# Reordering the head of an attention-plus-feed-forward kernel: states ahead of masks, outputs in their own banks, first rows by token blocks

## The chip, the cores and the metric

One core of a Trainium2 chip. The metric is device time in microseconds (us); a run gives one time, and its profile gives a span that is some 2 us shorter (205.6 us for a run of 207.38). Each milestone below is read from the trace of one execution.

## The reference

Linear attention with decay over blocks of 64 tokens, whose output goes into a GELU feed-forward layer.

```python
# attention: B=4, H=8, S=768, D=64
for b in range(S // 64):
    intra = (qb @ kb.T * Dmask) @ vb
    inter = (qb * lam_pow) @ kv_state
    out[b] = intra + inter
    kv_state = lam_block * kv_state + (kb * rev_pow).T @ vb
# feed-forward: x (3072 x 512), w_in (512 x 2048), w_out (2048 x 512)
out = gelu_tanh(x @ w_in) @ w_out
```

## The kernel before

The kernel walks through 24 steps, each of 256 tokens of four heads. Two steps (the two halves of the heads) make 256 rows of the feed-forward layer's input. The helpers that matter:

```python
def scores(n):   ...  # TensorE: q.k of step n into the bank pair Sps
def causal(n):   ...  # VectorE: PT = Sps * mask                        (1.22 us)
def products(n, s, banks=None, evacuate=True):
    # TensorE. n: k.v of step n into columns 256.. of two banks OK[0], OK[1]
    #          s: outputs of step s (PT.v, then q.state) into columns 0..255
    ...
def x_out(s, OK): ... # ScalarE: two copies OK[c] -> xT, the feed-forward input
def update(s, c, parts="tu"):
    # "t", VectorE: state t = t_old * lamu + OK[c][:, 256:384]  (two instructions)
    # "u", GpSimd:  u = t with the other head masked out
def cast_win(j, lo, hi, w, cs, on_act): ...  # w_in from fp32 to fp16, VectorE or ScalarE
def fill(n): ...      # TensorE: the next n pieces of feed-forward work
```

A *row* of the feed-forward layer below (rows 0 to 3, rows 4 to 7) is not a token: it is one block of 128 of the 2048 hidden features, computed in one PSUM bank. A *chunk* is 128 of the layer's 512 inputs, and a *token block* is 256 of the 512 rows of `x` that come first. *Cover* is the TensorE work that runs while another engine's copy is under way.

Every engine executes its instructions in the order of the program. A bank that VectorE (a state) and ScalarE (a copy) both read is handed over by semaphores, one reader after the other. The stretch that the change reorders, before:

```python
    update(1, 0)
    idle(3)
    scores(2)
    products(2, None)
    causal(2)
    prep_v(3)
    update(2, 0)
    update(1, 1)
    update(2, 1, "t")
    idle(2)
    stage_t(3)
    OK1 = products(None, 1, evacuate=False)[0]
    OK2 = products(None, 2, evacuate=False)[0]   # new banks
    x_out(2, OK2)
    x_out(1, OK1)
    scores(3)
    banks = products(3, None)
    update(3, 0)
    cast_win(0, 0, 256, 128, c01)                 # rows 0 and 1, VectorE
    cast_win(0, 256, 512, 256, c01, on_act=True)  # rows 2 and 3, ScalarE
    causal(3)
    queue_group(0)
    fill(4)                                       # rows 0-3, chunks 0 and 1
    products(None, 3, banks)
    cast_win(0, 0, 512, 256, c23)
    fill(8)                                       # rows 0-3, chunks 2 and 3, by token block
    # ... rows 4 to 7, 8 to 15, w_out, then steps 4 to 23
```

Later, nine more pieces of fill, then `prep(4)` (VectorE multiplies step 4's query by its decay, ScalarE casts its keys) and `stage_t(4)`, TensorE's transposes of both.

## Time and profile before

| | before |
|---|---|
| time, median of 3 runs (of 4 with the later rounds) | 207.87 us (207.69) |
| all four | 207.36 to 208.07 us |
| TensorE busy | 197.1 of 205.6 us |
| step 2's scores begin | 13.63 us |
| first feed-forward row begins | 18.15 us |
| rows 4 to 7 begin | 22.54 us |
| step 4's transposes begin | 40.67 us |

Read such a kernel by the matmul starts. TensorE is 96% busy, so an edit that removes no matmuls can only close holes between them. The prediction shows where the holes are. The table's last four rows are starts of single TensorE instructions; they are the milestones.

### The profile page before, as it was taken

To read this page: it belongs to the slowest core of one execution; us is meant where nothing else is said; L and a number is where in the kernel's file an instruction comes from. 1 tells how busy PE (TensorE), PEld (TensorE's weight loads), DVE (VectorE), ACT (ScalarE), POOL (GpSimd) and SP (SyncE) were. 2 spreads that over 40 slices of the span, in tenths; PEclk is the share of its full clock that TensorE was granted. 3 is DMA by queue.
4 is the path that set the end of the run, shared out by engine and by line. 5 is a ranking of instruction groups with operands and counts; after the bars stand their busy time and mean duration, and the time that the engine had idled before them with its cause. 6 is when DMAs were issued, how large, how long until landed. Compare 5 with 4: busy or idle time off the path is not lost.

```text
span 205.6 us, 5583 instructions
## 1 busy us (share of the span) xinstructions
PE 197.1 (96%) x2321; PEld 128.0 (62%) x2321; DVE 144.4 (70%) x271; ACT 108.1 (53%) x204; POOL 69.9 (34%) x80
## 2 busy tenths in 40 slices
PE   7988999999999999999999999999999999999990
PEld 2554644456875788644788554788555888446880
DVE  4788627867699998929997639996559474056631
ACT  2355778475882573487541577442676323665110
POOL 5495123646586851326224403404420110000000
PEclk9999999999999999999999999999999999999999
DMA  5999999999999998996549981736320003300033
GB/s 137 298 322 387 387 387 376 277 291 332 333 248 243 294 235 154 202 279 161 141 102 274 230 234 50 190 70 156 103 54 0 3 0 105 104 0 0 3 102 102
DMA packets 64057, 37.85 MB, mean 184 GB/s; under 512 B 17696, under 2 KB 59168, under 8 KB 64032
## 3 DMA queue, kind: packets, MB, share of 16 engines
q1 hardware_dynamic: 63760, 37.24, 66.9%
q8 instruction: 18, 0.29, 0.6%
q10 hardware_dynamic: 272, 0.26, 0.4%
q14 instruction: 7, 0.06, 0.1%
HBM read 27.27 MB, written 6.29 MB: 163 GB/s over the span
## 4 chain that ended last, share of the span: by engine, by line
PE 91%; DVE 2%; DMA 2%; issue 1%; ACT 1%; DVEq 0%
PE Hps L401 35%; PE O2ps L416 10%; PE MB L469 8%; PE MA L469 7%; PE MD L469 7%; PE Sps L271 4%; PE MC L469 4%; PE Hps L514 4%; PE OK L329 3%; PE idle L573 3%; PE OK L320 3%; PE Tps L242 2%; DMA qkT<-qk 2%; PE OK L306 1%; DVE t L366 1%
## 5 line engine op out<-in xcount | busy, mean ns | idle before, releaser
L401 PE MATMUL Hps<-xT,w_in 128*128 128x512 f16 (+1 forms) x416 | 79.1, 346 | 0.0
L405 ACT ACTIVATE gT<-Hps 128x512 f16<-128x512 f32 x88 | 52.3, 597 | 22.6 <-PE Hps L401 21.8
L401 PEld LDWEIGHTS <-w_in 128*128 128x128 f16 x416 | 40.2, 98 | 33.5
L373 POOL TENSOR_TENSOR u<-t,lumask 128x256 f16<-128x256 f32 x40 | 31.4, 791 | 80.9 <-DVE t L366 54.2
L446 DVE TENSOR_TENSOR gs<-gT 128x512 f16<-128x512 f16 (+1 forms) x70 | 36.6, 586 | 10.8 <-ACT gT L405 10.6
L280 DVE TENSOR_TENSOR PT<-Sps,mask 128x1024 f16<-128x1024 f32 x24 | 29.2, 1217 | 17.3 <-PE Sps L271 17.2
L469 PEld LDWEIGHTS <-gs 128*128 128x128 f16 x360 | 34.9, 98 | 4.0
L211 POOL TENSOR_TENSOR v<-v,dv 128x512 f16<-128x512 f32 x24 | 29.2, 1219 | 4.7 <-DMA v<-in_v_dram 4.7
L343 ACT ACTIVATE xT<-OK 128x256 f16<-128x256 f32 x48 | 18.2, 453 | 20.0 <-PE OK L329 16.5
L416 PE MATMUL O2ps<-w_out,gT 128*128 128x512 f16 x96 | 21.9, 379 | 0.0
L476 ACT ACTIVATE m<-MB 128x512 f32<-128x512 f32 x9 | 5.4, 597 | 28.1 <-PE MB L469 28.1
L226 ACT ACTIVATE qk<-k 128x512 f16<-128x512 f32 x24 | 15.0, 624 | 8.8 <-DMA k<-in_k_dram 8.8
L221 DVE TENSOR_TENSOR qk<-q,dq 128x512 f16<-128x512 f32 x23 | 19.2, 834 | 0.0
L469 PE MATMUL MA<-w_sum,gT 128*128 128x256 f16 x144 | 17.5, 273 | 0.1
L469 PE MATMUL MD<-w_sum,gs 128*128 128x256 f16 x136 | 17.5, 273 | 0.0
L469 PE MATMUL MB<-w_out,gs 128*128 128x256 f16 x144 | 17.2, 273 | 0.0
L366 DVE SCALAR_TENSOR_TENSOR t<-t,lamu,OK 128x64 f32<-128x64 f32 x64 | 14.5, 273 | 2.1 <-PE OK L306 0.9
L480 DVE TENSOR_TENSOR o<-MA,m 128x512 f32<-128x512 f32 x9 | 6.2, 688 | 13.9 <-ACT m L476 13.9
L469 PEld LDWEIGHTS <-gT 128*128 128x128 f16 x144 | 14.0, 98 | 2.8 <-ACT gT L405 0.3
L416 PEld LDWEIGHTS <-gT 128*128 128x128 f16 x96 | 9.2, 98 | 9.9
L271 PEld LDWEIGHTS <-qkT 64*64 64x64 f16 x384 | 6.1, 106 | 8.3 <-issue 4.2
L123 DVE TENSOR_TENSOR w_sum<-wo,wo 128x1024 f16<-128x1024 f32 x6 | 7.9, 1362 | 4.2 <-DMA wo<-in_moe_w_out_dram 4.2
(55 smaller groups left out, 169.2 us busy)
## 6 DMA issues: line engine op xcount, KB each, us to landing
q<-in_q_dram SPq DMA_DIRECT2D x24, 256.0 KB, 4.5
k<-in_k_dram SPq DMA_DIRECT2D x24, 256.0 KB, 5.0
v<-in_v_dram SPq DMA_DIRECT2D x24, 256.0 KB, 4.9
out_dram<-o SPq DMA_DIRECT2D x22, 256.0 KB, 3.4
wo<-in_moe_w_out_dram SPq DMA_DIRECT2D x4, 1024.0 KB, 9.2
wi<-in_moe_w_in_dram SPq DMA_DIRECT2D x4, 512.0 KB, 8.0
wi<-in_moe_w_in_dram SPq DMA_DIRECT2D x2, 1024.0 KB, 12.5
out_dram<-o SPq DMA_DIRECT2D x2, 128.0 KB, 2.2
```

What stands on the lines that cost most here:

```text
L211: pin(nc.gpsimd.tensor_tensor(wide(tv[:]), ld32[s][2][:], decay(dv, s), ALU.mult))
L221: pin(q_eng.tensor_tensor(wide(tq), q32[:], decay(dq, s), ALU.mult))
L226: pin(nc.scalar.activation(out=wide(tk), in_=k32[:], func=AF.Copy))
L280: pin(nc.vector.tensor_tensor(t[:].rearrange("p a b c d -> p (a b) (c d)"), Ss.pop(n)[:].rearrange("p a b c d -> p (a b) (c d)"), mask[:]. ...
L343: pin(nc.scalar.activation(out=dst[:, :, c * P : (c + 1) * P].rearrange("p hp (t j) -> p hp j t", j=2), in_=OK[c][:, 0:256].rearrange("p ( ...
L366: pin(nc.vector.scalar_tensor_tensor(t[:, hp, :], state[half][:, hp, :], lamu[:, 2 * half + hp : 2 * half + hp + 1], K[:, hp, :], ALU.mult ...
L373: pin(nc.gpsimd.tensor_tensor(u[:], state[half][:].unsqueeze(2).to_broadcast([P, 2, 2, D]), lumask[:, 2 * half : 2 * half + 2, :].unsqueez ...
L401: pin(nc.tensor.matmul(by_block(Hps[:, i, :]), w_in16[:, c, f * P : (f + 1) * P], x(c), start=(c == 0), stop=(c == NC - 1)))
L405: pin(nc.scalar.activation(out=dst, in_=Hps[:], func=AF.Gelu_apprx_tanh))
L416: pin(nc.tensor.matmul(O2[tau][0][:], gT[:, f % HF, f // HF, tau * P : (tau + 1) * P], w_out16[:, f, :], start=(n == 0), stop=(n == NF - 1)))
L446: pin(nc.vector.tensor_tensor(gsum[m][:, i, :], block(T0, F0, i), block(T1, F1, i), op))
L469: pin(nc.tensor.matmul(dst, lhsT, rhs, start=(i == 0), stop=(i == HF - 1), skip_group_check=True))
```

## The change

The intent: free VectorE, which carries the chain of waits twice in this stretch. Step 1's second state and step 2's first state go ahead of step 2's mask; step 2's outputs go into the banks that already hold its k.v; the first four feed-forward rows are cut by token block, so that each block can start when its inputs are there; the first weight casts go ahead of step 3's first state (they were ahead of its mask already). Step 3's outputs move behind four of the matmuls on chunks 2 and 3, so that four matmuls instead of eight are left to cover their copies. One later cast goes to ScalarE, and half of step 3's transposes and the second copy of its outputs go to VectorE.

```diff
-        if s == 2:                                   # evacuation of the transposes
+        if s in (2, 3):                              # half on ScalarE, half on VectorE
 ...
-    def x_out(s, OK):
+    def x_out(s, OK, second=None):                   # second copy on another engine
 ...
-            for fs, stages in ((range(4), (((0, 1), both, False), ((2, 3), b0, False),
-                                           ((2, 3), b1, True))),
+            for fs, stages in ((range(4), (((0, 1), b0, False), ((0, 1), b1, False),
+                                           ((2, 3), b0, False), ((2, 3), b1, True))),
 ...
     update(1, 0)
+    update(1, 1, "t")
     idle(3)
     scores(2)
-    products(2, None)
+    banks = products(2, None)
+    update(2, 0)
     causal(2)
     prep_v(3)
-    update(2, 0)
-    update(1, 1)
-    update(2, 1, "t")
+    update(1, 1, "u")
     idle(2)
     stage_t(3)
-    OK1 = products(None, 1, evacuate=False)[0]
-    OK2 = products(None, 2, evacuate=False)[0]
-    x_out(2, OK2)
-    x_out(1, OK1)
+    products(None, 1)
+    products(None, 2, banks)
+    update(2, 1, "t")
     scores(3)
     banks = products(3, None)
-    update(3, 0)
     c01, c23 = slice(0, 2), slice(2, 4)
     cast_win(0, 0, 256, 128, c01)
     cast_win(0, 256, 512, 256, c01, on_act=True)
+    update(3, 0)
     causal(3)
     queue_group(0)
-    fill(4)
-    products(None, 3, banks)
-    cast_win(0, 0, 512, 256, c23)
     fill(8)
+    cast_win(0, 0, 256, 256, c23, on_act=True)
+    cast_win(0, 256, 512, 256, c23)
+    fill(2)
+    products(None, 3, banks, evacuate=False)
+    x_out(3, banks[0], nc.vector)
+    fill(6)
+    update(3, 1, "t")
     cast_win(1, 0, 512, 256, c01)
-    update(3, 1, "t")
     cast_win(1, 0, 512, 256, c23)
```

More of the change, by code (lines that the diff above doesn't have):

```diff
@@ L244, in stage_t @@
         o = qkp.tile([P, 2, 2, 2, P], FP16, tag="qkT", name=f"qkT_{s}")
-        if s == 2:
+        if s in (2, 3):
             pin(nc.scalar.activation(out=o[:, 0], in_=Tps[:, 0], func=AF.Copy))
             pin(nc.vector.tensor_copy(out=o[:, 1], in_=Tps[:, 1]))
-        elif s in (1, 3, 5, 6):
+        elif s in (1, 5, 6):
             pin(nc.scalar.activation(out=o[:], in_=Tps[:], func=AF.Copy))
@@ L342, in x_out @@
         for c in range(2):
-            pin(nc.scalar.activation(
-                out=dst[:, :, c * P : (c + 1) * P].rearrange("p hp (t j) -> p hp j t", j=2),
-                in_=OK[c][:, 0:256].rearrange("p (hp j t) -> p hp j t", hp=2, j=2),
-                func=AF.Copy))
+            d = dst[:, :, c * P : (c + 1) * P].rearrange("p hp (t j) -> p hp j t", j=2)
+            o = OK[c][:, 0:256].rearrange("p (hp j t) -> p hp j t", hp=2, j=2)
+            if c == 1 and second is not None:
+                pin(second.tensor_copy(out=d, in_=o))
+            else:
+                pin(nc.scalar.activation(out=d, in_=o, func=AF.Copy))
     us = {}
@@ L509, in mm1_part @@
         def mm1_part(f, cs, blocks, last):
-            if cs[0] == 0:
+            opens = f not in first
+            if opens:
                 first[f] = ps_M.tile([P, N], FP32, tag="M", name="Hps")
@@ L515, in mm1_part @@
                                      w_in16[:, c, f * P : (f + 1) * P], x(c)[:, blocks],
-                                     start=(c == 0), stop=last and c == NC - 1,
+                                     start=opens and c == 0, stop=last and c == NC - 1,
                                      skip_group_check=True))
```

## The prediction

> **What bounds the kernel now.** I read the page's busy shares first, then the chain of waits in order of time, then the timeline of the first 25 us engine by engine, then the waits between 12 and 41 us. The page says that TensorE is the kernel:
>
> ```profile
> PE 197.1 (96%) x2321; PEld 128.0 (62%) x2321; DVE 144.4 (70%) x271; ACT 108.1 (53%) x204; POOL 69.9 (34%) x80
> ```
>
> A span of 205.6 less 197.1 leaves 8.5 us in which TensorE is idle. About 1.4 us of it lies before its first instruction and some 5 us after its last matmul, so about 2 us is left, and nearly all of it comes before 19 us. The chain of waits, between 13 and 21 us, shows where (start, length, what):
>
> ```profile
> 13.59 0.04 issue
> 13.63 0.45 PE Sps L271 x16
> ...
> 15.25 0.36 DVE t L366 x2
> 15.61 0.02 issue
> 15.63 0.48 DVE t L366 x2
> 16.11 0.04 issue
> 16.15 0.41 PE OK L320 x15
> ...
> 17.42 0.47 DVE t L366 x2
> 17.89 0.21 DVE w_in L107
> 18.10 0.05 issue
> 18.15 0.60 PE Hps L514 x2
> 18.75 0.04 issue
> 18.79 1.47 PE Hps L514 x6
> ```
>
> The reader is to see that VectorE carries the chain twice: the state of step 1 (`t`, 15.63) holds back step 2's outputs at 16.15, and the state of step 3 (17.42) plus a weight cast hold back the first feed-forward row at 18.15. The TensorE and VectorE timelines give the sizes:
>
> ```profile
> 18.15 2.11 PE L514 MATMUL Hps<-xT,w_in 128*128 128x512 f16 x8 [0.79 <-DVE w_in L107]
> ...
> 17.80 0.93 DVE L107 CAST w_in<-wi 128x256 f16<-128x256 f32 x2
> ...
> 20.86 0.76 ACT L343 ACTIVATE xT<-OK 128x256 f16<-128x256 f32 x2 [2.20 <-PE OK L329]
> ...
> 21.71 0.47 DVE L366 SCALAR_TENSOR_TENSOR t<-t,lamu,OK 128x64 f32<-128x64 f32 x2 [0.51 <-issue]
> ```
>
> From matmul start to matmul start I find four holes after 15 us that a new order could close: 0.19 us at 15.5, 0.32 at 15.8, 0.79 at 17.4 and 0.20 at 18.6, together 1.5 us. After 18.8 us TensorE streams back to back until one hole of 0.2 us at 77 us, which comes from ScalarE's order there. So the change, which lies wholly before 24 us, is worth what it moves the start of that stream, and never more than 1.5 us of 207.9, or 0.7%.
>
> **What the Trainium skill says.** (1) "PSUM — Partial Sum Buffer", section "PSUM bank collisions raise a hardware error", says that any two engines on one bank and quadrant collide, ScalarE reading against VectorE reading included, so that access is guarded by bank. This kernel's build does so, and the trace agrees: the `t` at 21.71 shares its bank with the second `xT` copy of ScalarE, which ends at 21.62, and starts 0.09 us later. (2) "SBUF — State Buffer", section "Who interferes with whom", says that a VectorE cast in a two-port mode and a GpSimd instruction exclude each other. The trace agrees: of the two casts at 17.80 the first took 0.29 us and the second, beside GpSimd's `u` at 17.97, took 0.72. (3) "TensorE: Matmul & The Clock Gate", section "Wait — 56ns, not 53.3ns?", gives N / 2.4 GHz + 2.5 ns between warm matmuls. Here it is 0.216 us at 512 columns and 0.109 at 256, so a row split in two pays some 2 ns for each added matmul.
>
> **The change part by part.** I carried the new instruction order of each engine through with these durations, and 0.05 to 0.09 us for each hand-over, as the trace has them.
>
> State of step 1 ahead of the mask. Its two `t` instructions go to 13.89 (the copy at 13.50 takes 0.28, and its reader follows 0.1 later), and the first state of step 2 to 14.27 to 14.72, since its products end at 14.17. The mask of step 2 then runs 14.64 to 15.86, where it was 14.11 to 15.33. Step 2's outputs now wait for that mask alone, since they go into banks that they already have: 15.92, where they were held to 16.15. That is 0.23 us earlier. Six `t` instructions leave the stretch behind the mask, but half a microsecond of them goes in front of it, so only half of the 0.5 us of holes there is won. The key transposes of step 3 are not in the way: ScalarE's half 15.20 to 15.80, then VectorE's half to 16.24, because they share a bank. Done alone by ScalarE they took to 16.22.
>
> Scores of step 3: 16.59 (was 16.82). Its products end at 17.13 (was 17.36).
>
> ScalarE copies step 1's outputs at 15.78 and 16.10, and step 2's at 16.59 and 16.91, ending at 17.35 (was 18.20). That is 0.85 us won, but off the path. Its weight cast starts at 17.3 instead of 18.01.
>
> VectorE now has the second state of step 2 ahead of the first weight casts. That `t` reads the bank that ScalarE copies until 17.35, so by the bank rule it starts at 17.44 and ends at 17.91. The casts come at 17.83 and 18.04, and now no `u` lies beside them (the next waits for step 3's state), so both should take 0.29. First feed-forward row: 17.83 + 0.29 + 0.05 = 18.17, where it was 18.15. The 0.23 us won is lost here, to a wait that takes the place of the one removed. The second row comes at 18.39, without the 0.20 us hole.
>
> From there: 16 matmuls of 0.109 are 1.75, to 19.92; four more on chunks 2 and 3 make 20.36. ScalarE's cast for those needs the second part of the weights, which landed at 18.61 in the trace; it runs 18.66 to 19.31, in time. Step 3's outputs, 0.58 plus 0.09 for the switch, end at 21.03 (was 20.77). Only four matmuls, 0.44 us, now lie behind them, to 21.47, where eight and 0.87 us did. The second token block needs both copies of step 3's outputs: ScalarE's half 21.12 to 21.58 and VectorE's half 21.24 to 21.64, so it starts at 21.70, a new hole of 0.23 us. Eight matmuls later, at 22.57, rows 4 to 7 begin. Before it was 22.54. VectorE's casts for rows 4 and 5 follow its copy and the last state, and end at 22.52, just in time.
>
> Sum: -0.20 (second row) + 0.02 (first row) + 0.23 (wait for step 3's copies), and the rest in rounding: about 0.0 us. All matmuls are the same work, with 8 more starts of about 2 ns, and 8 more weight loads of 98 ns that lie under matmuls of 109 ns.
>
> **The rivals.** (a) The new order closes the hole: if the second state of step 2 does not wait for ScalarE's copy, the casts start when the weights land (17.26), and the row starts near 17.65; with the late hole smaller too, 0.5 us is won at 22 us. The banks' rule and the 21.71 wait speak against it, and even then the next rival takes part of it back. (b) A fixed arrival caps any gain. The DMA queue is full from 3 us to beyond 45 us, so landings do not move with TensorE:
>
> ```profile
> 38.77 1.50 DVE L221 TENSOR_TENSOR qk<-q,dq 128x512 f16<-128x512 f32 x1
> ...
> 40.46 0.59 PEld L242 LDWEIGHTS <-qk 128*128 128x128 f16 x7
> 40.67 0.50 PE L242 MATMUL Tps<-ident,qk 128*128 128x128 f16 x6
> ```
>
> Step 4's query ends at 40.27 on VectorE, behind sums that started when a weight landed at 32.1, and TensorE takes it at 40.46. An earlier TensorE would wait there: of any gain only 0.15 to 0.3 us can pass. For (a) this makes 207.55 to 207.7. (c) The split rows and the smaller cover behind step 3's outputs cost more than I count, or VectorE's casts for rows 4 to 7 come late (they follow one copy and one state, and the second of them lies beside GpSimd's `u`, where such a cast took 0.84): 0.3 us lost, 208.2. Nothing later gives it back, since TensorE has no later idle time to absorb it.
>
> **Range and chances.** The mean of the three is close to no change: 207.87 + 0.0 by my sum, a little less for (a) under the cap of (b), which I hold likelier than (c) since the last wait is worked out from overlapping copies and may be 0.1 shorter. I take 207.75. The before runs spread over 0.56 us by themselves, which is wider than the effect, so 8 times in 10 it should be within 207.3 to 208.25. A gain of over 2% needs 4.2 us, nearly three times all the holes that the change can reach: 0.01. A loss of over 2% would need a wait of 4 us that nothing shows: 0.01. Within 2%: 0.98.
>
> **What would show it.** In the changed profile: step 2's outputs near 15.9 and scores of step 3 near 16.6; the second state of step 2 just behind the end of ScalarE's fourth copy (about 17.4); the first feed-forward row at 18.1 to 18.2, with both casts at 0.29; a hole of about 0.2 us ahead of the second token block near 21.6; rows 4 to 7 at 22.4 to 22.7; no hole at the transposes of step 4 near 40.5. If the first row starts at 17.7, rival (a) holds and I then expect TensorE to wait for the query at 40.3. If holes appear at 22.6 to 24, rival (c) holds. The prediction is wrong if the time moves by more than 0.6 us either way, which would need a wait outside the first 24 us.

## The result, and the profile after

The changed kernel took 207.74 us (median of 4, 207.47 to 208.02) against 207.69 for the kernel before (median of 4, 207.36 to 208.07). The ratio is 1.0002, with a 95% interval of 0.9977 to 1.0027: the same. Ratios here and below are the mean time of one kernel's fast runs over that of the other's in the same rounds, so they are not quite the ratios of the medians quoted beside them.

The page's busy shares of the changed kernel: TensorE has eight more matmuls (the split rows), VectorE one instruction more (two copies more, one cast less).

```profile
PE 196.8 (96%) x2329; PEld 128.4 (62%) x2329; DVE 144.8 (70%) x272; ACT 108.1 (53%) x204; POOL 70.1 (34%) x80
```

The chain of waits of the changed kernel in the same stretch (start, length, what):

```profile
14.79 1.14 DVE PT L280
15.93 0.04 issue
15.98 0.42 PE OK L320 x16
16.39 0.23 PE OK L329 x2
16.62 0.02 issue
16.65 0.77 ACT xT L348 x2
17.42 0.04 DVEq L368
17.46 0.04 issue
17.50 0.47 DVE t L368 x2
17.97 0.21 DVE w_in L107
18.19 0.05 issue
18.23 2.36 PE Hps L517 x20
20.59 0.35 PE OK L320 x16
20.94 0.34 PE OK L329 x4
21.28 0.02 issue
21.30 0.46 DVE xT L346
21.76 0.05 issue
21.80 2.34 PE Hps L517 x14
```

Where step 2's outputs (15.98) waited for a state before, they now wait for the mask alone, and step 3's scores follow sooner. But the chain no longer goes from TensorE to VectorE. It goes through ScalarE's copies of those outputs (16.65), then a state on VectorE (17.50), then the cast, then the first row (18.23). The VectorE timeline and its waits say the same with the length of the wait:

```profile
17.50 0.47 DVE L368 SCALAR_TENSOR_TENSOR t<-t,lamu,OK 128x64 f32<-128x64 f32 x2 [1.16 <-ACT xT L348]
17.89 0.49 DVE L107 CAST w_in<-wi 128x256 f16<-128x256 f32 x2
```

VectorE is idle for 1.16 us ahead of the state. The state reads columns 256 to 383 of the bank and the copy columns 0 to 255, so what ties them is the bank and not the data. The two casts behind it take 0.49 us together, where one of them took 0.72 alone before, so rows 0 to 3 now run without a hole (20 matmuls in 2.36 us). The second new hole is at the end of the chain: the second token block (21.80) waits for VectorE's copy of step 3's outputs.

The runs differ in when step 2's scores begin, from 13.32 to 14.19 us, although TensorE has the same instructions up to there in every kernel here. So I count the milestones from that start. All numbers in us, from the start times of single TensorE instructions. A hole is the time between two matmul starts above their usual spacing; the brackets of the views count idle time from the modelled end of the matmul before, and so are smaller (0.30 for a hole of 0.46).

| after step 2's scores | before | changed |
|---|---|---|
| step 2's outputs, first | 2.13 (but 15 of 16 wait to 2.51) | 2.25 |
| step 3's scores | 3.19 | 2.93 |
| first feed-forward row | 4.51 | 4.51 |
| step 3's outputs | 6.55 | 6.80 |
| hole ahead of the second token block | none | 0.27 |
| rows 4 to 7 | 8.91 | 8.97 |
| step 4's transposes | 27.04 | 27.10 |
| last matmul | 186.66 | 186.72 |

From step 4's transposes to the last matmul both take 159.62 us. Everything that the change did is over at rows 4 to 7, where it is 0.06 us behind.

### The profile page after: what moved, and what is told of

It reads as the page before. It is cut to its first block, busy times and chain, and to the rows that moved or that the text cites. A ratio compares the mean times of both kernels' runs of the same rounds, so it can differ in the third digit from the quotient of the medians.

```text
span 205.8 us, 5599 instructions
## 1 busy us (share of the span) xinstructions
PE 196.8 (96%) x2329; PEld 128.4 (62%) x2329; DVE 144.8 (70%) x272; ACT 108.1 (53%) x204; POOL 70.1 (34%) x80
## 4 chain that ended last, share of the span: by engine, by line
PE 88%; DMA 3%; SPq 2%; DVE 2%; ACT 2%; issue 1%; DVEq 0%
PE Hps L403 37%; PE O2ps L418 10%; PE MB L471 8%; PE MA L471 7%; PE MD L471 7%; PE MC L471 4%; PE Sps L271 3%; PE Hps L517 3%; PE OK L329 3%; DMA k<-in_k_dram 3%; PE OK L320 3%; SPq L68 2%; PE Tps L242 1%; PE OK L306 1%; ACT xT L348 1%; DVE t L368 1%
```

## The experiments

Theory A: the change wins where it was meant to, and pays it back by two waits, namely the state that waits for ScalarE's copy in the same bank (with the casts queued up behind it), and the thin cover behind step 3's outputs. Theory B: even if these were mended, a later arrival (step 4's query) would cap the gain. Theory C: the first row is bound by something else, such as the landing of the weights. Each run has a profile, and all were correct.

**The state behind the casts.** One line of the changed kernel moved.

```diff
     products(None, 2, banks)
-    update(2, 1, "t")
     scores(3)
     banks = products(3, None)
     cast_win(0, 0, 256, 128, c01)
+    update(2, 1, "t")
```

> The changed kernel with one line moved: the second state of step 2 goes behind the first two weight casts instead of ahead of them. Theory A (that state waits for ScalarE's copy of the same bank and holds the casts back): the first feed-forward row starts when the weights have landed and been cast, 0.5 to 0.6 us earlier after the scores of step 2 (3.9 to 4.0 us instead of 4.51), the hole after step 3's outputs stays at 0.2 to 0.3 us, rows 4 to 7 begin 0.5 to 0.6 us earlier, and the transposes of step 4 pass on 0.4 to 0.5 of that; time 0.3 to 0.5 us below the changed kernel. Theory B (an arrival later on caps every gain): first row earlier as in A, but the transposes of step 4 move by less than 0.2 us and the time stays. Theory C (the casts wait for something else, such as the weights' arrival): the first row does not move by more than 0.1 us.

Measured: 207.17 us (median of 6) against 207.38 before (11 runs); ratio 0.9983, interval 0.9968 to 0.9998. The first row starts at 3.58, rows 4 to 7 at 8.24 (0.73 earlier than in the changed kernel), the last matmul at 186.21 (0.51 earlier, and 0.45 earlier than in the kernel before; the interval of the ratio is 0.04 to 0.66 us). The VectorE timeline of this run:

```profile
17.03 0.71 DVE L107 CAST w_in<-wi 128x256 f16<-128x256 f32 x2 [0.40 <-DMA wi<-in_moe_w_in_dram]
17.80 0.86 DVE L368 SCALAR_TENSOR_TENSOR t<-t,lamu,OK 128x64 f32<-128x64 f32 x4
```

The casts now start as the weights land (17.00). Theory A's first wait is shown: one line in the program's order was worth 0.93 us at the first row, counted from step 2's scores. More than I expected, because scores of step 2 came 0.3 us later in this run than in the changed kernel's while the weights landed 0.2 us earlier; by the clock from the span's start the row came 0.64 us earlier (17.59 against 18.23). C is refuted for the changed kernel. In the six traces in which the state still stands ahead of the casts and the rest of the new head is in place, the first row comes at 4.51 each time, while the weights land anywhere from 16.93 to 17.40; only with the state out of the way can the landing bound the row.

At rows 4 to 7 the gain is 0.73 and not 0.93, because a hole of 0.19 us opens at 18.23, ahead of row 2: ScalarE casts the weights of rows 2 and 3 behind its fourth copy, from 17.55 to 18.17.

```profile
17.55 0.62 ACT L105 ACTIVATE w_in<-wi 128x512 f16<-128x512 f32 x1
```

Theory B, that step 4's transposes move by less than 0.2 us, is wrong: they move by 0.52. A part of it is right: of the 0.73 us at rows 4 to 7, 0.51 arrive. The rest is a wait at step 4's transposes, in the weight-load timeline of this run:

```profile
40.59 0.28 PEld L242 LDWEIGHTS <-qk 128*128 128x128 f16 x5 [0.54 <-DVE qk L221]
```

The query ended on VectorE at 40.53. Between rows 4 to 7 and these transposes lie 18.13 us in the kernel before and in the changed one, and 18.34 here: 0.21 us of TensorE's time was lost. The query's load is not the whole of this cap. It landed at 38.83, and VectorE's multiply of it then took 1.52 us (39.01 to 40.53), beside GpSimd's cast of `w_out` (38.01 to 39.99); the same multiply for step 5 took 0.68. In all 13 traces step 4's takes 1.25 to 1.52. No run here moved that cast, so what this would win is not shown.

**The same, with the transposes asked for later.** First attempt.

```diff
-    fill(9)
+    fill(10)
     prep(4)
     stage_t(4)
     prep(5)
-    fill(2)
+    fill(1)
```

> The run with the state behind the casts, and beside it one more piece of four feed-forward matmuls placed ahead of step 4's transposes instead of behind them, so that TensorE asks for step 4's query 0.86 us later. Theory A without a cap: the same end as the run with the state behind the casts alone, within 0.1 us in the trace. Theory B (the query's arrival on VectorE caps the gain): the last matmul comes 0.1 to 0.4 us earlier than in that run, and there is no wait at the transposes. If the shorter cover behind the transposes (0.86 instead of 1.73 us) is too short, the scores of step 4 wait for the copy of the transposes, up to 0.2 us.

Measured: 208.22 us (median of 6), ratio 1.0029 (1.0013 to 1.0045): a miss. The tenth piece completes an output, and its copy then stands ahead of the cast of step 4's keys in ScalarE's order:

```profile
41.55 0.60 ACT L424 ACTIVATE o<-O2ps 128x512 f32<-128x512 f32 x1 [2.78 <-PE O2ps L418]
...
42.05 1.14 ACT L226 ACTIVATE qk<-k 128x512 f16<-128x512 f32 x2
42.72 0.23 PEld L242 LDWEIGHTS <-qk 128*128 128x128 f16 x4 [1.16 <-ACT qk L226]
```

ScalarE waits for that output, and the keys behind it, so the second half of the transposes comes 1.14 us late. I made the edit blind to what one piece brings along; it is mended below.

**More cover behind step 3's outputs.**

```diff
     fill(8)
     cast_win(0, 0, 256, 256, c23, on_act=True)
     cast_win(0, 256, 512, 256, c23)
-    fill(2)
     products(None, 3, banks, evacuate=False)
     x_out(3, banks[0], nc.vector)
-    fill(6)
+    fill(8)
```

> The changed kernel with step 3's outputs placed four matmuls earlier, so that eight matmuls instead of four lie between them and the second token block. Theory A: the hole of 0.27 us behind step 3's outputs shrinks to below 0.05 us, rows 4 to 7 begin 0.15 to 0.27 us earlier; the outputs start within 0.1 us of the end of the mask of step 3, so up to 0.1 us may be lost there. Time 0.1 to 0.3 us lower, not to be told from none by the time alone. Rival: the second block waits for its weights' cast and not for the copies of step 3; then the hole stays.

Measured: 207.43 us (median of 4), ratio 0.9992 (0.9973 to 1.001), not to be told from none by the time. In the trace the hole is gone, rows 4 to 7 begin at 8.69 (0.28 earlier) and the last matmul at 186.45 (0.27 earlier). Theory A's second wait is shown, and worth all of its 0.27 us.

**The second copy back on ScalarE.**

```diff
-    x_out(3, banks[0], nc.vector)
+    x_out(3, banks[0])
```

> The changed kernel with the second copy of step 3's outputs back on ScalarE. Theory A: the copies end 0.2 us later (one after the other on ScalarE, 0.32 us apart, instead of side by side), the hole behind step 3's outputs grows from 0.27 to 0.4 to 0.5 us, and the last state of step 3 waits for ScalarE; rows 4 to 7 begin 0.1 to 0.3 us later. Rival (the hole comes from something else): hole and rows 4 to 7 unchanged within 0.05 us.

Measured: one run, 208.66 us. The hole is 0.46 us and rows 4 to 7 begin at 9.18, 0.21 later, as theory A has it. The end was 0.79 us later than in the changed kernel, which the edit doesn't explain. One load of weights (the fourth) landed at 23.20 us, where in every other run it landed between 20.9 and 21.5, and all later loads came late with it; step 4's query ended at 41.90 and TensorE waited 0.56 us for it. Hence a second run of the same kernel:

> The run with the second copy on ScalarE again, because in its trace one load of weights landed 1.7 us late, ahead of anything that the edit touches, and the end with it. Theory A: hole behind step 3's outputs 0.46 us again and rows 4 to 7 0.21 us later than in the changed kernel; the end 0.2 us later if the loads land as in the other runs, and over 0.5 us later only if the late landing comes back with the edit.

Measured: 208.22 us. Hole 0.46, rows 4 to 7 at 9.19, no wait at the transposes, last matmul at 186.95: 0.23 later than in the changed kernel. The late load did not come back with the edit. Its time of 208.22 is not 0.23 above the changed kernel's median but 0.48; in this run the scores of step 2 began at 14.19 us, 0.47 later than in the changed kernel's profile. TensorE and ScalarE timelines of this run, to be read with 21.80 in the changed kernel:

```profile
22.48 1.72 PE L517 MATMUL Hps<-xT,w_in 128*128 128x256 f16 x11 [0.30 <-ACT xT L348]
...
21.67 0.76 ACT L348 ACTIVATE xT<-OK 128x256 f16<-128x256 f32 x2 [2.75 <-PE OK L329]
```

**Only the casts' place, on the kernel before.**

```diff
     banks = products(3, None)
-    update(3, 0)
     cast_win(0, 0, 256, 128, c01)
     cast_win(0, 256, 512, 256, c01, on_act=True)
+    update(3, 0)
```

> The kernel before with one line moved: the first weight casts ahead of the first state of step 3, nothing else of the change. Theory A (the casts' place on VectorE sets the first row, and in the changed kernel the wait for ScalarE's copy ate this part's gain): the first row starts 0.4 to 0.6 us earlier after the scores of step 2 than in the kernel before (3.9 to 4.1 us instead of 4.51), the second row without its 0.2 us hole, rows 3 and 4 held by ScalarE's cast as before; rows 4 to 7 begin 0.4 to 0.6 us earlier (8.3 to 8.5 instead of 8.91), and the end in the trace moves by 0.2 to 0.5 us, less where the query of step 4 comes late. Rival (the first row is bound by the weights' arrival or by the copies on ScalarE): row and end unchanged within 0.1 us.

Measured: 207.07 us (median of 4) against 207.49, ratio 0.9977 (0.9957 to 0.9998). First row at 4.12 (0.39 earlier, just outside what I expected), rows 4 to 7 at 8.40 (0.51 earlier), last matmul at 186.44 (0.22 earlier). Here too TensorE waits at step 4's transposes, 0.27 us. So this part of the change alone is a gain of half a microsecond at rows 4 to 7. VectorE's timeline shows the casts waiting for the weights to land:

```profile
17.34 0.49 DVE L107 CAST w_in<-wi 128x256 f16<-128x256 f32 x2 [0.93 <-DMA wi<-in_moe_w_in_dram]
```

**Only step 2's order, on the kernel before** (the split rows, the casts' order and the split evacuation of step 3's transposes stay as they were).

```diff
     update(1, 0)
+    update(1, 1, "t")
     idle(3)
     scores(2)
-    products(2, None)
+    banks2 = products(2, None)
+    update(2, 0)
     causal(2)
     prep_v(3)
-    update(2, 0)
-    update(1, 1)
-    update(2, 1, "t")
+    update(1, 1, "u")
     idle(2)
     stage_t(3)
-    OK1 = products(None, 1, evacuate=False)[0]
-    OK2 = products(None, 2, evacuate=False)[0]
-    x_out(2, OK2)
-    x_out(1, OK1)
+    products(None, 1)
+    products(None, 2, banks2)
+    update(2, 1, "t")
```

> The kernel before with only step 2's order changed: the state of step 1 and the first state of step 2 ahead of the mask, step 2's outputs in their own banks, its second state behind the outputs. Theory A: step 2's outputs and the scores of step 3 come 0.2 us earlier, as in the changed kernel, but the second state then waits for ScalarE's fourth copy, step 3's state and the casts queue up behind it, and the first row starts 0.4 to 0.8 us later than in the kernel before (4.9 to 5.3 us after the scores of step 2 instead of 4.51); rows 4 to 7 begin 0.3 to 0.8 us later. Rival (the own banks help by themselves): first row 0.2 us earlier.

Measured: one run of 207.47 us. Step 3's scores at 2.96 (0.23 earlier than before), but the first row at 5.06 (0.55 later), rows 4 to 7 at 9.25 (0.34 later), last matmul at 187.07 (0.41 later). The single time says nothing here, because step 2's scores began 0.31 us earlier in this run than in the kernel before. The VectorE timeline, then ScalarE's and GpSimd's of the same run:

```profile
17.27 0.86 DVE L366 SCALAR_TENSOR_TENSOR t<-t,lamu,OK 128x64 f32<-128x64 f32 x4 [1.71 <-POOL u L373]
...
15.81 1.37 ACT L343 ACTIVATE xT<-OK 128x256 f16<-128x256 f32 x4
...
16.11 0.61 POOL L373 TENSOR_TENSOR u<-t,lumask 128x256 f16<-128x256 f32 x1
```

A trap for the reader: the view puts the wait of 1.71 us down to GpSimd. But GpSimd's `u` was done at 16.72, and ScalarE's copies at 17.18, 0.09 us before the state starts. The instruction waits for both, and the one that ended last is ScalarE.

**The first rows whole again, on the changed kernel.**

```diff
-    ... (range(4), (((0, 1), b0, False), ((0, 1), b1, False), ((2, 3), b0, False), ((2, 3), b1, True))
+    ... (range(4), (((0, 1), both, False), ((2, 3), b0, False), ((2, 3), b1, True))
 ...
-    fill(8)
+    fill(4)
     cast_win(0, 0, 256, 256, c23, on_act=True)
```

> The changed kernel with the first four rows' chunks 0 and 1 over both token blocks at once, as before (four pieces of two matmuls of 512 columns instead of eight of 256). Theory A (step 2's copies, done at 17.4, are not what the first row waits for): nothing moves, first row and rows 4 to 7 within 0.06 us of the changed kernel. Rival (the split lets the first row start before step 2's copies are done, and is what holds the loss down): the first row or rows 4 to 7 come 0.2 us later or more.

Measured: 207.45 us in one run. First row 4.51, rows 4 to 7 at 8.95 (0.02 earlier). The split into token blocks does nothing here, because in the changed kernel the first row begins (18.23) long after step 2's copies end (17.41).

**The later transposes again, mended:** the keys' cast ahead of the extra piece.

```diff
     fill(9)
     prep(4)
+    fill(1)
     stage_t(4)
     prep(5)
-    fill(2)
+    fill(1)
```

On the changed kernel:

> The changed kernel with one piece of four feed-forward matmuls (0.86 us) taken from behind step 4's transposes and put ahead of them; unlike in the earlier run without a cap, the casts of step 4's keys now stand ahead of that piece, so that ScalarE does not put an output copy ahead of them. Theory A and B: the changed kernel does not wait at those transposes in its trace (slack 0.4 us), so with loads that land in time the end in the trace stays within 0.1 us; the slowest runs may become faster, since a late load no longer stops TensorE. Rival (the shorter cover behind the transposes costs): scores of step 4 wait 0.1 us or more, and the end comes later by that.

Measured: 207.55 us (median of 6, 207.2 to 208.53) against 207.67 (11 runs); ratio 0.9993 (0.9956 to 1.0029). The last matmul is at 186.84, 0.12 later than in the changed kernel; the rival's cost is real, though one step later than it said: step 5's transposes wait 0.18 us for its query, which stands behind the copy of step 4's transposes on VectorE. That the runs would scatter less was not seen.

With the state behind the casts:

> The state of step 2 behind the casts, together with that same move ahead of step 4's transposes. Theory B (step 4's query caps the gain): no wait at the transposes, where the run with the state behind the casts alone waited 0.21 us; so the whole 0.73 us won at rows 4 to 7 reaches the end: last matmul 0.65 to 0.75 us earlier than in the changed kernel, counted from the scores of step 2 (186.0 us instead of 186.72), and the time 0.2 to 0.4% below the kernel before. Without a cap there: the end as in the run with the state behind the casts alone, 186.2.

Measured: 207.21 us (median of 6); ratio 0.9973 (0.9936 to 1.0011; the kernel before had one run of 209.84 in these rounds, which widens all three intervals of this job). No wait at step 4's transposes, as expected. But the last matmul comes at 186.11, not at 186.0: of the 0.21 us 0.10 is won, since the wait at step 5, which cost 0.12 us at the end in the run before, is new here too.

**All three.** The run before this one with `fill(2)` moved behind step 3's outputs as in the run with more cover.

> The run before this one with, in addition, step 3's outputs four matmuls earlier, so that eight matmuls cover the copies. The hole of 0.27 us goes, but the outputs now wait for the mask of step 3, which ended 0.3 us ahead of them: rows 4 to 7 begin 0.05 to 0.1 us earlier than without it (8.15 to 8.2 us after the scores of step 2), the end likewise. If the mask is not what follows next, the whole 0.27 us is won (8.0).

Measured: 207.00 us (median of 6, 206.87 to 207.05); ratio 0.9961 (0.9927 to 0.9995). Rows 4 to 7 at 8.16, last matmul at 186.03. The mask of step 3 is indeed what follows: in this run's chain of waits the outputs start right behind it.

```profile
17.70 0.85 DVE t L368 x4
18.55 1.15 DVE PT L280
19.70 0.04 issue
19.74 0.42 PE OK L320 x16
```

This version beats the kernel before: 0.67 us below its median in the same rounds, and each of its six runs is below each of the eleven of the kernel before (without the run of 209.84 the mean is still 0.56 us lower). The changed kernel was not run in these rounds; against it the trace shows 0.69 us at the last matmul (186.03 against 186.72).

## Why the prediction was right

The time was predicted as no change (207.75 us, 0.98 for within 2%) and measured so (207.74, ratio 1.0002). Step by step, from the changed kernel's trace; all of it ran 0.09 us late against the trace before, from the scores of step 2 on, so a predicted start should be read with 0.09 added.

- Step 2's outputs at 15.92 and step 3's scores at 16.59, 0.23 us earlier than before: 15.98 and 16.65. Right. Counted from step 2's scores, step 3's come 0.26 us earlier.
- The split evacuation of step 3's transposes wins nothing by itself: VectorE's half ended at 16.34 instead of 16.24, since it lies behind the mask. Right in kind.
- The state of step 2 waits for ScalarE's fourth copy: predicted 17.35 for the copy's end and 17.44 for the state, measured 17.41 and 17.50. This was the step that the prediction stood on. The Trainium skill ("PSUM — Partial Sum Buffer", section "PSUM bank collisions raise a hardware error") says why two readers must be kept apart; the run with the state behind the casts shows what the order cost.
- First row at 18.17, second row without its hole: 18.23, and no hole. Right.
- Step 3's outputs at 20.45, a hole of 0.23 us, rows 4 to 7 at 22.57: 20.52, 0.27, 22.69. Right, the hole 0.04 larger.
- The sum of 0.0: +0.06 us at rows 4 to 7, and at the last matmul. The prediction's three terms make 0.05 and not 0.0. Its hole of 0.79 us at 17.4 is the view's idle time; from start to start it is 0.98, of which about 0.1 is usual after such small matmuls. Neither changes the argument.
- Rival (a), that the state does not wait, fell for the changed kernel. I had shaded the number to 207.75 for it, against 207.87 by the sum; that the median then fell on 207.74 is chance, as the runs spread over 0.55 us. Without the wait I had put the first row near 17.65; in the mended kernel it came at 17.59. By the clock rows 4 to 7 came 0.44 us earlier there (22.25 against 22.69), near the 0.5 that I gave; counted from step 2's scores it is 0.73, because these scores began 0.29 us later in that run and the loads did not.
- Rival (b), the cap: the changed kernel does not reach it, as predicted, but the mended one does. I put 0.15 to 0.3 us as what could pass. With the casts' place alone 0.22 passed of 0.51 won; with the state behind the casts 0.51 passed of 0.73. The slack that I read from one trace (query done at 40.27, its weight load at 40.46) varies from run to run, since landings and TensorE's head do not move together. And I took the query's late end for its place behind the sums, and overlooked that its multiply took 1.50 us in the line that I showed.
- Rival (c), late casts for rows 4 to 7: not seen. The last piece of the sum that was only argued beforehand, that split rows cost nothing, is shown by the run with whole rows (0.02 us).

Together the two runs with one part alone say how the change came to nothing. The casts' place is worth 0.51 us at rows 4 to 7; step 2's order costs 0.34 there; the thin cover behind step 3's outputs costs 0.27. The parts don't add exactly, since they share the same waits, but a gain and two losses of this size leave 0.10 us, against 0.06 measured.

What stays open: why the scores of step 2 begin anywhere between 13.32 and 14.19 us in kernels whose TensorE instructions are the same up to there. The latest start (14.19 us) goes with 0.95 us of idle time of TensorE between 8 and 10 us, where the kernel before has 0.34 us. The traces point to a load: step 0's values land at 6.33 to 6.87 us in the six traces whose scores begin at 13.32 to 13.72, and at 7.15 to 7.34 in the seven with 13.91 to 14.19. In the latest, TensorE waits 0.39 us at 8.58 for GpSimd's product of these values. That they go together is shown; that the load is the cause is not, since no run moved it.

## What to carry to other kernels

When an instruction moves, ask which of its waits were satisfied in its old place and are not in its new one. Here a state was cheap ahead of the outputs, and behind them it inherited a wait for another engine's copy in the same bank, and gave it on to all that stood behind it in VectorE's order. And before counting a gain at the head, look for the next thing that arrives by its own clock, such as a load, since a gain beyond its slack is waited away. Look also at how long the work between that arrival and TensorE takes, and what runs beside it.

## What the Trainium skill lacked or had wrong

- "TensorE: Matmul & The Clock Gate", section "Back-to-back issue gap", gives about 131 ns for each matmul of 512 columns in a stream of weight load and matmul pairs, and says that N / 2.4 + 2.5 over-counts there. Here it does not: in the kernel before 32 such pairs in a row take 7.07 us, and less the 0.38 of the last one that is 0.216 us for each of the other 31, which is the formula's value. The measurement decides.

```profile
26.00 7.07 PE L401 MATMUL Hps<-xT,w_in 128*128 128x512 f16 x32
```

- "PSUM — Partial Sum Buffer" states the rule for two readers of one bank but not its price. Here a tile read half by ScalarE and half by VectorE took 0.60 and then 0.42 us, one after the other, and 1.02 us by ScalarE alone: sharing one bank won nothing. For step 2's tile in the kernel before VectorE stood idle for 0.21 us until ScalarE's half was done (13.12). The hand-over from ScalarE to VectorE took up to 0.09 us (21.62 to 21.71, 17.41 to 17.50).
- No page that I read says that the loads and the engines' head drift apart from run to run. Step 2's scores began at 13.32 to 14.19 us while the first weights landed at 16.58 to 17.40, and one load in one run came 1.7 us late.
